# Two batches' kv products in one visit, twice, and a remainder tile drawn forward: attention and MLP in one Trainium2 kernel

## The chip, the cores and the metric

The kernel runs on one core of a Trainium2 chip. The metric is device microseconds (us) of one execution, as the median of several. The core has TensorE (PE in the profile, matrix products), VectorE (DVE), ScalarE (ACT), GpSimd (POOL), the sync engine (SP, which here only starts transfers) and 16 DMA engines, on which every transfer runs.

## The reference

For each of 8 batches and 8 heads of width 64, with 576 rows: an attention without a softmax, normalised by its root mean square, and then a block with a layer norm and two weights.

```python
kv  = einsum('bhsd,bhse->bhde', k, v)            # 64x64 per batch and head
o   = einsum('bhsd,bhde->bhse', q, kv)
x   = o / sqrt(mean(o*o, -1) + 1e-6) * g_norm    # then heads side by side: (8, 576, 512)
xn  = (x - mean(x)) / sqrt(var(x) + 1e-6) * g_ln
out = x + relu(xn @ w_ch1) @ w_ch2               # 512 -> 2048 -> 512
```

## The kernel before

**Tiles.** The 576 rows of a batch are four main tiles of 128 rows and a rest of 64. The rests of batches b-1 and b make one remainder tile, so there are four of them: 1, 3, 5 and 7, named by the higher batch (r1 to r7 below). The four remainder tiles are a ninth block of 512 rows, `"rem"`, that goes through the MLP last.

**Slots.** PE sets the pace. Its order is written out by hand: `mm1(b, 0, 4)` is 16 groups of four matmuls of 512 columns (a group fills one PSUM tile `p1`, of which there are three, and ACT evicts it with a relu at L419 into `m1`), and `mm2(b)` is four rows `ts` of 16 matmuls, each row in one of two PSUM tiles `p2`, which `finish` empties on DVE (L437) and stores through SP (L452, L453). Before each group of mm1 and each four matmuls of mm2 stands a `tick()`: this is a slot. From batch 3 on, batch b has mm1 in slots 32b to 32b+15 and mm2 in 32b+16 to 32b+31; `"rem"` has 256 to 287. Whatever else is to be done is entered with `at(slot, fn)`, and all its instructions are put on all engines' queues when that tick is reached. A slot thus fixes an order of instructions, not a time: POOL and SP, which have little to do, often reach an instruction long before PE reaches the slot it was entered at.

**What is entered at slots.**

- `load_batches` (POOL): first one or two 1x1 copies into `gate`, which wait for a transfer that has to come before, and then two DMAs for each tensor named. `k_in`, `v_in` and `q_in` have two buffers each, for even and odd batches.
- `turn_q_dma(b)`: DVE copies q of a batch into `q_p` in another order (L204), and SP starts one DMA transpose of it into `qt` (L206). `qt` has four buffers.
- `kv_of(*bs)`: 40 matmuls on PE for each batch into the one PSUM tile `kv_ps` (L247), and then two copies on ACT for each batch (L252, L253) into `kv_pack[b % 4]`.
- `plan_tile(s, make, turn_at, on_pe, x_at)` carries one tile through. At slot s: `o` (PE, L274, reads `qt` and `kv_pack`, writes one of two PSUM tiles `o_ps`), `sq` (ACT, L280), `red` (DVE, L301). At x_at, s+2 if it isn't given: `root` (ACT, L311), `inv`, `y` (DVE, L306, after which `o_ps` is free), `x`, `xc` (DVE, L325 to L335). At x_at+4: `var` (ACT, L343). At turn_at: a DMA transpose from SP into the block's `xT_blk` (L355), which mm1 reads.
- `rem_tile(b)` makes the remainder tile out of `qt` and `kv_pack` of batches b-1 and b.

mm1 of a batch can't start before the `xT_blk` of its four tiles has landed.

Of the kernel before, what the change touches and what calls it, by code (L numbers as in the profile page):

```python
# [14 lines left out]
def kernel(  # L15
# [18 lines left out]
    B, H, S, D = q.shape  # L34
# [57 lines left out]
    def load(dst, t, b, h0=0, h1=H):  # L92
        nc.gpsimd.dma_start(dst[:64, h0:h1], lo(t, b, h0, h1))
        nc.gpsimd.dma_start(dst[64:, h0:h1, :J], up(t, b, h0, h1))

    def load_batches(what, *after):
        for element in after:
            nc.gpsimd.tensor_copy(gate, element)  # L98
        tensors = {"k": (k_in, k), "v": (v_in, v), "q": (q_in, q)}
        for name, b in what:  # L100
            dst, src = tensors[name]
            load(dst[b % NB], src, b)
# [63 lines left out]
    qts, held, blks, rstds, m1s, q_ps = {}, {}, {}, {}, {}, {}  # L166
# [35 lines left out]
    def turn_q_dma(b):  # L202
        q_p = kv_in.tile([128, JJ, H, D], bf16, tag="qp", bufs=2)
        nc.vector.tensor_copy(q_p.rearrange("p j h d -> p h j d"), q_in[b % NB])  # L204
        q_t = qt_pool.tile([128, JJ, HP, 128], bf16, tag="qt", name="qt")
        nc.sync.dma_start_transpose(  # L206
            q_t.rearrange("p j hp t -> p (j hp) t"), q_p.rearrange("p j h d -> p (j h d)"))
        qts[b] = q_t
# [31 lines left out]
    def kv_of(*bs):  # L240
        kv_ps = ps_m.tile([128, len(bs), HP, D], f32, tag="misc", name="kv_ps")
        for i, b in enumerate(bs):
            for hp in range(HP):
                for j in range(JJ):
                    for hh in range(2):
                        h = 2 * hp + hh
                        nc.tensor.matmul(  # L247
                            kv_ps[hh * D:hh * D + D, i, hp, :], lhsT=k_in[b % NB][:, h, j, :],
                            rhs=v_in[b % NB][:, h, j, :], start=(j == 0), stop=(j == JJ - 1))
        for i, b in enumerate(bs):  # L250
            kvp = held[b] = kv_pack[b % 4]
            nc.scalar.copy(kvp[:D, :, :D], kv_ps[:D, i])  # L252
            nc.scalar.copy(kvp[D:, :, D:], kv_ps[D:, i])  # L253

    def new_block(n, bufs):
        x_blk = xpool.tile([128, 4, Dm], f32, tag=f"x{n}", bufs=bufs, name="x_blk")
        st_blk = xpool.tile([128, 3, 4], f32, tag=f"st{n}", bufs=bufs, name="st_blk")
        xT_blk = xpool.tile([128, nK, 512], bf16, tag=f"xT{n}", bufs=bufs, name="xT_blk")
        return x_blk, st_blk, xT_blk
# [98 lines left out]
    def main_tile(b, j, pool=None, tag="ops"):  # L358
        q_t, kvp = qts[b], held[b]
        if b not in blks:  # L360
            blks[b] = new_block("main", 3)
        return Tile([(slice(0, 128), lambda hp: q_t[:, j, hp, :], kvp)], blks[b], j, pool, tag)

    def rem_tile(b):
        mms = []
        for half, bb in enumerate((b - 1, b)):
            qt, kp = qts.pop(bb), held.pop(bb)
            mms.append((slice(half * 64, (half + 1) * 64),
                        lambda hp, qt=qt: qt[:, J, hp, :64], kp))
        if "rem" not in blks:  # L370
            blks["rem"] = new_block("rem", 1)
        return Tile(mms, blks["rem"], b // 2)

    def plan_tile(s, make, turn_at, on_pe, x_at=None):
        box = []

        def first():
            t = make()
            box.append(t)
            t.o()  # L380
            t.sq()
            t.red()

        def second():
            t = box[0]
            t.y()
            t.x()
            t.xc()

        def third():  # L390
            box[0].var()

        def fourth():
            box[0].turn(on_pe)

        at(s, first)
        at(x_at or s + 2, second)
        at((x_at or s + 2) + 4, third)
        at(turn_at, fourth)
# [22 lines left out]
    def rstd_of(b):  # L422
        rstd = work.tile([128, 4], f32, tag="rstd", bufs=3, name="rstd")
        nc.scalar.activation(rstd, blks[b][1][:, 2, :], func=AF.Sqrt, scale=1.0 / Dm, bias=eps_sb)  # L424
        nc.vector.reciprocal(rstd, rstd)  # L425
        rstds[b] = rstd
# [47 lines left out]
    def at(slot, fn):  # L474
        agenda.setdefault(int(slot), []).append((slot, fn))
# [162 lines left out]
    def turned_q(b):  # L638
        return qts[b][:1, J, HP - 1, 127:]

    at(47, lambda: load_batches((("k", 3), ("v", 3), ("q", 3)), turned_q(2)))
    at(68, lambda: load_batches((("k", 4), ("v", 4), ("q", 4)),
                                turned_q(3), blks[2][2][:1, nK - 1, 511:]))
    at(100, lambda: load_batches((("k", 5), ("v", 5), ("q", 5)), turned_q(4)))
    at(132, lambda: load_batches((("q", 6), ("k", 6), ("v", 6), ("k", 7), ("v", 7)),
                                 turned_q(5)))
    at(164, lambda: load_batches((("q", 7),), turned_q(6)))


    at(115, lambda: kv_of(5))  # L650
    for s, bs, rem, x_at, tn in ((56, (3,), 1, 64, 69), (85, (4,), 3, 88, 94),
                                 (152, (6, 7), 5, 154, 160)):
        at(s, lambda bs=bs: kv_of(*bs))
        plan_tile(s + .1, lambda rem=rem: rem_tile(rem), tn, False, x_at)
    plan_tile(210, lambda: rem_tile(7), 216, False)


    for b, at_q, at_o, step in ((3, 56.05, 67, 4.3), (4, 86, 97, 4.75),
                                *((b, 32 * b - 43.3, 32 * b - 32, 5) for b in range(5, B))):
        at(at_q, lambda b=b: turn_q_dma(b))  # L660
        for j in range(J):
            o = at_o + step * j
            plan_tile(o, lambda b=b, j=j: main_tile(b, j), o + 6, False)
        at(32 * b + 14, lambda b=b: rstd_of(b))
# [59 lines left out]
```

## Time and profile before

| | |
|---|---|
| median of 3 runs | 288.96 us (288.90 to 289.06) |
| the profiled execution's own time | 288.75 us |
| its span, first to last instruction | 286.7 us |
| around the span | 2.05 us |
| PE busy | 277.8 us, 97% of the span |
| DVE, ACT, POOL busy | 150.0, 152.9, 43.1 us |
| read from HBM, written | 36.71 MB, 9.44 MB |

Times in the views are microseconds from the start of the span. In the chain that ended last, every piece has its start, its length, and the engine with the tile written and the source line; "issue" is time in which nothing that the profile shows was waited for. In a timeline, the bracket at the end of a row says how long the engine had stood idle before it, and for whom. A DMA's row in a timeline is its issue; the time from there to landing is in the view of DMAs.

### The profile page before, as it was taken

Reading aid. Unit: us, or ns where it says so; the run is one execution under the profiler, and the core shown is the slowest. Engines: PE = TensorE matmul, PEld = TensorE weight load, DVE = VectorE, ACT = ScalarE, POOL = GpSimd, SP = SyncE. Lnnn points to the kernel's source line nnn. Section 1 sums busy time; section 2 is a strip of 40 time slices with the busy share of each in tenths; the row PEclk is TensorE's granted clock in tenths of the full one; section 3 lists DMA queues with packets and bytes.
Section 4 is the critical chain, followed back from the end, with each engine's and each line's share of the span. In section 5 each row is a group of like instructions: output and inputs, shape, how many; then the busy total and the mean of one; then the engine's idle time right before and its main releaser. Section 6 shows DMA issues by size and latency. Waiting matters only on the chain.

```text
span 286.7 us, 5727 instructions
## 1 busy us (share of the span) xinstructions
PE 277.8 (97%) x2269; PEld 158.0 (55%) x2295; DVE 150.0 (52%) x331; ACT 152.9 (53%) x333; POOL 43.1 (15%) x73
## 2 busy tenths in 40 slices
PE   7889999999999999999999999999999999999995
PEld 3579755995579654454444544444444444444444
DVE  5774119937997883774376475763679200220022
ACT  3477844995468643971387338911893066016500
POOL 8522510041036005000710020000000000000000
PEclk9999999999999999999999999999999999999999
DMA  7999999969997979986999995047203410230033
GB/s 215 198 209 202 201 191 197 214 111 188 144 180 124 185 141 172 214 101 127 159 215 190 120 160 135 18 82 158 56 18 72 95 37 0 48 81 19 0 73 76
DMA packets 67419, 36.76 MB, mean 128 GB/s; under 512 B 35517, under 2 KB 62525, under 8 KB 67393
## 3 DMA queue, kind: packets, MB, share of 16 engines
q0 software_dynamic: 28720, 18.29, 44.2%
q1 hardware_dynamic: 38160, 17.39, 30.4%
q10 hardware_dynamic: 512, 0.72, 0.8%
q8 instruction: 18, 0.29, 0.5%
q14 instruction: 9, 0.07, 0.1%
HBM read 36.71 MB, written 9.44 MB: 161 GB/s over the span
## 4 chain that ended last, share of the span: by engine, by line
PE 91%; DMA 2%; DVE 2%; ACT 2%; issue 1%; DVEq 0%; POOLq 0%
PE p L432 43%; PE p L416 42%; PE o_ps L274 3%; DMA v_in<-in_v_dram 2%; PE kv_ps L247 2%; ACT m L419 1%; DVE x_blk L292 0%; DVE xc L552 0%; ACT xT_blk L353 0%; PE tp L351 0%; ACT rms L311 0%; PE odd L226 0%; DVE ss L518 0%; PE tp L559 0%; DVE ss L301 0%
## 5 line engine op out<-in xcount | busy, mean ns | idle before, releaser
L416 PE MATMUL p<-xT_blk,w_sb 128*128 128x128 bf16 (+2 forms) x1015 | 131.2, 285 | 0.9
L432 PE MATMUL p<-w_sb,m 128*128 128x512 bf16 (+2 forms) x592 | 126.2, 368 | 1.2 <-issue 0.5
L419 ACT ACTIVATE m<-p 128x512 bf16<-128x512 f32 x144 | 85.2, 596 | 46.7 <-PE p L416 44.3
L416 PEld LDWEIGHTS <-w_sb 128*128 128x128 bf16 x1024 | 78.6, 98 | 44.5 <-issue 1.1
L432 PEld LDWEIGHTS <-m 128*128 128x128 bf16 x608 | 57.3, 98 | 62.9
L437 DVE SCALAR_TENSOR_TENSOR o_sb<-p,rstd,x_blk 128x512 f32<-128x512 f32 (+2 forms) x38 | 27.2, 721 | 47.7 <-PE p L432 42.1
L280 ACT ACTIVATE sq<-o_ps 128x512 f32<-128x512 f32 x35 | 20.9, 596 | 26.7 <-PE o_ps L274 26.5
L343 ACT ACTIVATE dev<-x_blk,st_blk 128x512 f32<-128x512 f32 x36 | 25.7, 714 | 13.1 <-DVE st_blk L329 13.1
L301 DVE TENSOR_REDUCE ss<-sq 128x8 f32<-128x512 f32 x35 | 23.7, 678 | 17.0 <-ACT sq L280 17.0
L335 DVE SCALAR_TENSOR_TENSOR xc<-x_blk,st_blk,g_ln_sb 128x512 bf16<-128x512 f32 x34 | 25.6, 752 | 1.2
L306 DVE TENSOR_TENSOR y<-o_ps,inv 128x512 f32<-128x512 f32 x33 | 22.8, 692 | 3.1
L325 DVE SCALAR_TENSOR_TENSOR x_blk<-y,g_norm_sb 128x512 f32<-128x512 f32 x33 | 22.8, 692 | 1.1
L318 DVE RECIPROCAL inv<-rms 128x8 f32<-128x8 f32 x36 | 7.3, 202 | 23.3 <-ACT rms L311 23.3
L425 DVE RECIPROCAL rstd<-rstd 128x4 f32<-128x4 f32 x9 | 1.6, 175 | 29.9 <-ACT rstd L424 29.8
L311 ACT ACTIVATE rms<-ss,eps_sb 128x8 f32<-128x8 f32 x36 | 10.6, 295 | 11.5 <-DVE ss L301 11.3
L274 PEld LDWEIGHTS <-qt 128*128 128x128 bf16 (+1 forms) x156 | 10.3, 100 | 6.0 <-issue 0.4
L274 PE MATMUL o_ps<-kv_pack,qt 128*128 128x128 bf16 (+1 forms) x156 | 13.6, 220 | 0.0
L98 POOL COPY gate<-qt 1x1 bf16<-1x1 bf16 x5 | 0.9, 177 | 82.4 <-DMA qt<-q_p 82.4
L199 PE MATMUL p<-fill_sb 128*128 128x512 bf16 x26 | 7.8, 452 | 1.3 <-DVE eps_sb L138 1.2
L252 ACT CAST kv_pack<-kv_ps 64x256 bf16<-64x256 f32 x7 | 2.6, 366 | 10.7 <-PE kv_ps L247 10.7
L343 ACT ACTIVATION_READ_ACCUMULATOR dev<-x_blk,st_blk 128x1 f32 x36 | 6.8, 190 | 0.0
L247 PEld LDWEIGHTS <-k_in 128*64 128x64 bf16 x280 | 4.9, 112 | 2.4 <-issue 2.3
(82 smaller groups left out, 112.6 us busy)
## 6 DMA issues: line engine op xcount, KB each, us to landing
out_dram<-o_sb SPq DMA_DIRECT2D x66, 128.0 KB, 2.6
w_sb<-in_moe_w_ch_dram POOLq DMA_DIRECT2D x8, 512.0 KB, 15.2
q_in<-in_q_dram POOLq DMA_DIRECT2D x7, 320.0 KB, 9.7
k_in<-in_k_dram POOLq DMA_DIRECT2D x7, 320.0 KB, 8.7
v_in<-in_v_dram POOLq DMA_DIRECT2D x7, 320.0 KB, 10.3
q_in<-in_q_dram POOLq DMA_DIRECT2D x8, 256.0 KB, 10.5
k_in<-in_k_dram POOLq DMA_DIRECT2D x7, 256.0 KB, 9.3
v_in<-in_v_dram POOLq DMA_DIRECT2D x7, 256.0 KB, 12.3
```

The lines of the kernel that those rows point to most:

```text
L247: nc.tensor.matmul(kv_ps[hh * D:hh * D + D, i, hp, :], lhsT=k_in[b % NB][:, h, j, :], rhs=v_in[b % NB][:, h, j, :], start=(j == 0), stop=( ...
L274: nc.tensor.matmul(flat[rows, hp * 128:(hp + 1) * 128], lhsT=lhsT_of(hp), rhs=kvp[:, hp, :], start=True, stop=True)
L280: nc.scalar.activation(self.sq_t, self.o_ps, func=AF.Square)
L301: nc.vector.tensor_reduce(self.ss, self.sq_t, axis=AX.X, op=ALU.add)
L306: nc.vector.tensor_mul(self.y_t, self.o_ps, self.inv().to_broadcast([128, H, D]))
L325: nc.vector.scalar_tensor_tensor(x_blk[:, ts].rearrange("p (h d) -> p h d", h=H), in0=self.y_t, scalar=1.0, in1=g_norm_sb.to_broadcast([12 ...
L335: nc.vector.scalar_tensor_tensor(self.xc_t, in0=x_blk[:, self.ts], scalar=st[:, 1, self.ts:self.ts + 1], in1=g_ln_sb, op0=ALU.add, op1=ALU ...
L343: nc.scalar.activation(dev, x_blk[:, ts], func=AF.Square, bias=st[:, 1, ts:ts + 1], accum_out=st[:, 2, ts:ts + 1])
L416: nc.tensor.matmul(p1[:, i, :], lhsT=w1_sb[:, kk, de * 128:(de + 1) * 128], rhs=blk[2][:, kk, sl], start=(kk == 0), stop=(kk == nK - 1))
L419: nc.scalar.activation(m1[:, de0:de0 + per, sl], p1, func=AF.Relu)
L432: nc.tensor.matmul(p2[:, c0:c1], lhsT=m1s[b][:, de, ts * 128:(ts + 1) * 128], rhs=w2_sb[:, de, c0:c1], start=(de == 0), stop=(de == nDe - 1))
L437: nc.vector.scalar_tensor_tensor(o_sb[:, c0:c1], in0=p2[:, c0:c1], scalar=rstds[b][:, ts:ts + 1], in1=blks[b][0][:, ts, c0:c1], op0=ALU.mu ...
```

## The change

Batch 5's kv product is no longer made by itself at slot 115: it is made with batch 4's, at slot 93 instead of 85, and r3 moves with it. The products of 6 and 7 move from slot 152, in mm2 of batch 4, to slot 161, in mm1 of batch 5, with 7 made ahead of 6; r5 moves with them, and r7 follows it there instead of standing at slot 210. k and v of batch 5 are loaded behind q of 4, k and v of 6 behind q of 5, and q of 7 together with q of 6. The q turns of batches 4, 6 and 7 move from slots 86, 148.7 and 180.7 to 92, 147 and 151, and the main tiles of batch 4 from 97 and steps of 4.75 to 101 and steps of 4.3, those of 6 from 160 and steps of 5 to 165 and steps of 4.5. `rem_tile` keeps the q and kv of its two batches until later where they are those of r7. The number of instructions on PE is the same; POOL has one gate copy less.

```diff
@@ rem_tile @@
-            qt, kp = qts.pop(bb), held.pop(bb)
+            qt, kp = qts[bb], held[bb]
+            if b < B - 1:
+                del qts[bb], held[bb]
@@ kernel body @@
-    at(68, lambda: load_batches((("k", 4), ("v", 4), ("q", 4)),
+    at(68, lambda: load_batches((("k", 4), ("v", 4), ("q", 4), ("k", 5), ("v", 5)),
                                 turned_q(3), blks[2][2][:1, nK - 1, 511:]))
-    at(100, lambda: load_batches((("k", 5), ("v", 5), ("q", 5)), turned_q(4)))
-    at(132, lambda: load_batches((("q", 6), ("k", 6), ("v", 6), ("k", 7), ("v", 7)),
+    at(101, lambda: load_batches((("q", 5), ("k", 6), ("v", 6)), turned_q(4)))
+    at(132, lambda: load_batches((("q", 6), ("q", 7), ("k", 7), ("v", 7)),
                                  turned_q(5)))
-    at(164, lambda: load_batches((("q", 7),), turned_q(6)))

-    at(115, lambda: kv_of(5))
-    for s, bs, rem, x_at, tn in ((56, (3,), 1, 64, 69), (85, (4,), 3, 88, 94),
-                                 (152, (6, 7), 5, 154, 160)):
+    for s, bs, rem, x_at, tn in ((56, (3,), 1, 64, 69), (93, (4, 5), 3, 95, 101),
+                                 (161, (7, 6), 5, 162, 168)):
         at(s, lambda bs=bs: kv_of(*bs))
         plan_tile(s + .1, lambda rem=rem: rem_tile(rem), tn, False, x_at)
-    plan_tile(210, lambda: rem_tile(7), 216, False)
+    plan_tile(161.2, lambda: rem_tile(7), 170, False, 164)

-    for b, at_q, at_o, step in ((3, 56.05, 67, 4.3), (4, 86, 97, 4.75),
-                                *((b, 32 * b - 43.3, 32 * b - 32, 5) for b in range(5, B))):
+    for b, at_q, at_o, step in ((3, 56.05, 67, 4.3), (4, 92, 101, 4.3),
+                                (5, 116.7, 128, 5), (6, 147, 165, 4.5), (7, 151, 192, 5)):
         at(at_q, lambda b=b: turn_q_dma(b))
```

## The prediction

> **What bounds the kernel now.** I read the page's busy times first, then the chain that ended last, then the timelines of ACT, DVE and POOL around the pieces that move. TensorE is the bound, and nearly all of the chain is its own:
>
> ```profile
> PE 277.8 (97%) x2269; PEld 158.0 (55%) x2295; DVE 150.0 (52%) x331; ACT 152.9 (53%) x333; POOL 43.1 (15%) x73
> ...
> PE 91%; DMA 2%; DVE 2%; ACT 2%; issue 1%; DVEq 0%; POOLq 0%
> ```
>
> From 33 us on PE hardly stops. So work taken off ACT, DVE or DMA gains nothing; only PE work taken away gains, and every wait that reaches PE is paid in full. A 512-column matmul costs 0.2158 us: mm2(5), which has nothing entered in it, starts at 185.11 in the chain and ends at 198.92, 13.81 us for 64. A slot is four, 0.863 us. The pieces that the change moves stand in the chain thus:
>
> ```profile
> 100.21 0.75 PE kv_ps L247 x40
> 100.96 0.23 PE o_ps L274 x8
> 101.19 0.16 issue
> ...
> 128.08 0.75 PE kv_ps L247 x40
> 128.84 0.16 issue
> ...
> 161.78 1.39 PE kv_ps L247 x80
> 163.16 0.23 PE o_ps L274 x8
> 163.39 0.32 PE p L432
> ...
> 215.36 0.34 PE o_ps L274 x8
> ```
>
> Here kv of 4 with r3, kv of 5, kv of 6 and 7 with r5, and r7. None waits for anything: 80 matmuls for two batches cost 1.39 us, 40 cost 0.75 and a gap of 0.16 behind them.
>
> What lies behind a kv product is in ACT's timeline, four copies that start 0.05 us after the last matmul and end at 164.72:
>
> ```profile
> 163.21 0.37 ACT L252 CAST kv_pack<-kv_ps 64x256 bf16<-64x256 f32 x1 [3.95 <-PE kv_ps L247]
> 163.58 0.37 ACT L253 CAST kv_pack<-kv_ps 64x256 bf16<-64x256 f32 x1
> 163.97 0.37 ACT L252 CAST kv_pack<-kv_ps 64x256 bf16<-64x256 f32 x1
> 164.35 0.37 ACT L253 CAST kv_pack<-kv_ps 64x256 bf16<-64x256 f32 x1
> ```
>
> The first two aren't earlier than the other batch's matmuls. Nobody waits for them now: r5 reads kv of 4 and 5, and batch 6 is read at 170.40.
>
> The load of k, v and q of batch 4 is issued from 88.22 (POOL's timeline), and its last half is issued at 91.61 and lands 10.6 us later, at 102.2 (the view of DMAs for that moment). A load of five tensors, from 137.61, has its last half issued at 145.65 and landing 14.0 us later, at 159.65:
>
> ```profile
> 91.61 0.75 POOL L94 DMA_DIRECT2D q_in<-in_q_dram  x1
> ...
> q_in<-in_q_dram POOLq DMA_DIRECT2D x1, 256.0 KB, 10.6
> ...
> 145.65 0.68 POOL L94 DMA_DIRECT2D v_in<-in_v_dram  x1 [1.12 <-DMA q_in<-in_q_dram]
> ...
> v_in<-in_v_dram POOLq DMA_DIRECT2D x1, 256.0 KB, 14.0
> ```
>
> **What the Trainium skill says.** (1) "TensorE: Matmul & The Clock Gate", Part 2, step-by-step: only weight loads are pulled ahead, matmuls stay in program order. So a matmul that waits holds up everything behind it. The trace agrees with that page's 215.7 ns between 512-column matmuls (215.8 here). (2) "PSUM — Partial Sum Buffer", Engine vs sequencer instructions: ScalarE and VectorE are strict FIFO. The trace agrees: mm2(2)'s first row ends on PE near 99.4, and its finish starts on DVE at 100.97, straight behind tile (3,3)'s xc. (3) "DMA: Bandwidth & Descriptors", Issuing engines are not separate DMA queues: POOL's loads and SP's stores and transposes share the 16 engines. The trace agrees: 188 GB/s from 92 to 94 us with loads nearly alone, 184 from 94 to 96 with over a quarter of the bytes a transpose's.
>
> **The change part by part.**
>
> *Fewer visits: a gain of 0.6.* PE has the same instructions, so only the gaps go. By the chain the pieces cost now 1.13 (100.21 to 101.34), 0.92, 1.61 and 0.34, together 4.00. After: kv of 4 and 5 with r3 like the present pair, 1.61; the pair with r5, and r7 at 0.23, 1.84. That saves 0.55. By whole mm2 stretches against the empty one of 13.81 (14.90, 14.68, 15.53, 14.48 now) the pieces cost 4.35, and 1.72 and 1.95 after: 0.68. I take 0.6, ends 0.4 and 0.7.
>
> *kv of 5 at slot 93 waits for its load: +1.3.* Slot 80 starts at 95.89 and nothing is entered between it and slot 93 but a q copy on DVE, so slot 93 starts at 95.89 + 13 x 0.863 = 107.1, and the first matmul of batch 5 is due 0.7 later, at 107.8. k and v of 5 are queued straight behind q of 4 (POOL issues them from about 92.3 to 95; the buffers are long free). q of 4 lands at 102.2. In the load of five tensors the last two landed at 156.5 and 159.65, 6.4 us after the third (153.25), with transposes running beside them. 102.2 + 6.4 = 108.6. Beside them now run two stores of 0.26 MB, part of a third, and tile (3,3)'s transpose: a little over half a MB at some 190 GB/s would be 3 us if all were taken from the load, but the 6.4 already holds a share of such traffic. I take 109.1: PE waits 1.3. Ends: 0.3 (the DMA engines were idle in part from 102 to 107) and 2.6 (the same five-tensor load from its first issue, 22.0 us, gives 110.25). Behind it on PE is r3, mm2(2)'s last row and everything else.
>
> *Main tiles of 4 in steps of 4.3: +0.8.* The last `o` goes from slot 111.25 to 113, one slot into mm2(3), and the tiles follow each other in 4.3 slots, 3.93 us with the `o`. DVE needs 3.3 us for a tile, and about 1 us of idling for the `root` on ACT, which is in a queue with relus: 4.2, so it falls behind. The present steps of 4.3 (batch 3) show by how much (the chain, then DVE's timeline):
>
> ```profile
> 94.79 0.22 PE o_ps L274 x4
> ...
> 100.30 0.75 DVE L335 SCALAR_TENSOR_TENSOR xc<-x_blk,st_blk,g_ln_sb 128x512 bf16<-128x512 f32 x1
> 100.97 0.75 DVE L437 SCALAR_TENSOR_TENSOR o_sb<-p,rstd,x_blk 128x512 f32<-128x512 f32 x1
> ```
>
> From the end of `o` at 95.01 to the finish behind that tile's xc, 5.96 us; with steps of 4.75 (batch 4 now, `o` ends 124.63, finish 129.84) it was 5.21. In the new order the finish of mm2(3)'s first row stands behind xc of tile (4,3). It ends 5.96 + 0.75 = 6.7 us after `o`, and a little more (6.9 by laying out the rows in turn, as r3 is in this queue too). PE needs its p2 for the third row at slot 120, 7 slots or 6.04 us after `o`: a wait of 0.7 to 0.9. I take 0.8; ends 0.2 and 1.1.
>
> *r7 behind kv of 7 and 6: +1.4.* r7's first matmul reads kv_pack of 6, which ACT copies last. With the kv matmuls ending at 0, the copies end at 164.72 - 163.16 = 1.56 and PE sees it at 1.6; r5's `o` covers 0.23. PE waits 1.4. ACT has slot 160's relu (0.6) ahead of the copies, hidden by the 1.39 of kv. Ends 1.2 and 1.6: the order of rows leaves nothing else to run.
>
> *ACT and DVE in mm1(5): +1.0.* Now the visit is in mm2(4), where ACT has no relus. At slot 161 it has one per slot of 0.863 us (0.49 from start to start), and r5, r7 and tile (6,0) all come within four slots, each 1.5 us of ACT (sq 0.60, rms 0.20, var 0.70) and 3.3 us of DVE. From 0 as above, by the durations in the timelines: sq of r5 ends 2.2, red 2.9; sq of r7 2.8, red 3.6; DVE has r5's inv to xc from 3.8 to 6.4, r7's to 9.0, and only then red of (6,0), to 9.7. But ACT comes to rms of (6,0) at 8.3 and stands there until 9.75 with relus queued behind. PE has three p1: its group 170 could start at 10.1 and waits for relu 167 (to 10.6), group 171 for relu 168 behind var of r7, 172 for 169: 0.5 + 0.3 + 0.2 = 1.0. I take 1.0; ends 0 (rows a little shorter) and 1.7.
>
> *Costed at nothing.* q of 7 turned at 151: SP issues two q transposes of 3.2 us, with a pair of stores and tile (5,3)'s transpose between them. That one is issued about 4.5 us after q of 6 and lands 3.0 later, as now; by my layout about 1 us before slot 160 needs it. If that cover is gone PE waits up to 1 there. Loads of q 5, k 6, v 6 (gate at about 113) and q 6, q 7, k 7, v 7 (gate near 142, landed by 160) are needed from 131, 159 and 172. Stores queued behind q of 7 wait 3 us, and o_sb has four buffers. r7's old place at 210 and the last stretch have nothing that waits. r3's x at 95 is in DVE's queue ahead of batch 4.
>
> Sum: -0.6 + 1.3 + 0.8 + 1.4 + 1.0 = **+3.9**. Against the profiled execution, 286.7 + 2.05 = 288.75, that is 292.65; the median stands 0.2 higher, so 292.9.
>
> **The rivals.**
>
> *Only r7's wait is paid.* k and v of 5 arrive in time and the queues absorb the rest: +1.4 - 0.6 = +0.8, 289.8, and with one of the small waits up to 290.5. For it: 5 us with little DMA work from 102 to 107. Against: two tensors need 6.3 us at 188 GB/s alone.
>
> *The merge pays: faster.* PE saves the 0.6 to 0.7 of gaps: 288.3. It decides if the waits put in stay under 0.6 in all, at slot 161 above all: the copies there would have to be over about 0.8 us after the kv matmuls. For it: the copies of 7 are first, and could run under the matmuls of 6, and would take 0.7 out of the wait. Against: the pair now in the trace shows all four copies after the last matmul. Short of that it ends as no change.
>
> *A longer wait.* Loads and stores collide at slot 93 for over 3 us, or both q transposes delay (5,3). A fourth place, the TensorE page's Part 1, says that PE's clock falls to half after an idle window of about 3.4 us; no run here shows it (the granted clock is 1.00 everywhere). That would cost an estimated 1.7 more: +6 to +8, 295 to 297.
>
> **How the numbers follow.** No change is taken as within 0.2%, 0.6 us, about what a measurement of this kernel can tell. The forecast (two or more of the new waits) has 0.70, and its own terms at their ends, not all at once, give +1.8 to +6.5; r7's wait alone 0.16, of which 0.03 lies within 0.2%; the merge that pays 0.06, 0.04 faster and 0.02 within; the longer wait 0.08. So faster 0.04, within 0.2% 0.05, slower 0.91. For 8 in 10 the range goes from 289.9, which takes in most of the second case, to 295.6.
>
> **What would show it.** In the chain after: idle of PE at kv_ps near 107.8 for DMA v_in or k_in; at o_ps near 171 to 173 for ACT kv_pack, 1.4 us; p waiting for DVE o_sb near slot 120 and for ACT m in mm1(5). PE busy stays within 1 us of 277.8. It is wrong if L247 never waits, if r7 doesn't, or if PE stands for long anywhere else, at slot 160 above all.

## The result: slower by 3.4%, most of it in one wait

| | before | after |
|---|---|---|
| median of 4 runs | 288.93 us (288.52 to 289.06) | 298.77 us (297.74 to 299.51) |
| ratio, 95% interval | | 1.0341 (1.0306 to 1.0375) |
| the profiled execution, its span | 288.75, 286.7 us | 299.51, 297.4 us |
| PE busy | 277.8 us | 280.7 us |

Executions of the changed kernel differ by some us, since the wait at slot 93 and TensorE's clock behind it differ from one to the next. A number from one execution is therefore called that here, and a median stands beside it where the verdict needs it. A run over 1.5% above the shortest of its own kernel counts as slow and is left out of a ratio; two runs below are, both of "r7 out of slot 161" at 210.

The page after, the same two lines as before and the row of the clock (tenths of full speed, in 40 slices of 7.4 us):

```profile
PE 280.7 (94%) x2269; PEld 159.3 (54%) x2295; DVE 149.5 (50%) x331; ACT 152.4 (51%) x333; POOL 42.9 (14%) x72
...
PEclk9999999999999995999999999999999999999999
...
PE 77%; DMA 10%; DVE 6%; ACT 3%; issue 2%; POOL 0%; DVEq 0%; POOLq 0%
```

PE has the same 2269 matmuls, yet is busy 2.9 us longer, and its clock stands at a half in one slice. DMA has 10% of the chain instead of 2%. PE's waits, in us in total, times and longest (waits before 33 us, which both kernels have, left out):

```profile
PE kv_ps L247 <- DMA v_in<-in_v_dram: 5.5, 1, 5.5
PE o_ps L274 <- ACT kv_pack L253: 1.4, 1, 1.4
...
PE p L434 <- DVE o_sb L439: 0.7, 1, 0.7
...
PE p L418 <- ACT m L421: 0.5, 2, 0.3
```

These are the four places that the prediction named, and no fifth of that length. Their pieces in PE's timeline (`o`, mm1 and mm2 are now L274, L418 and L434):

```profile
107.21 0.82 PE L247 MATMUL kv_ps<-v_in,k_in 128*64 128x64 bf16 x40
113.50 1.28 PE L247 MATMUL kv_ps<-v_in,k_in 128*64 128x64 bf16 x40 [5.46 <-DMA v_in<-in_v_dram]
...
141.54 7.07 PE L434 MATMUL p<-w_sb,m 128*128 128x512 bf16 x31 [0.66 <-DVE o_sb L439]
...
180.97 0.41 PE L274 MATMUL o_ps<-kv_pack,qt 128*64 128x128 bf16 x8 [1.37 <-ACT kv_pack L253]
...
190.00 1.02 PE L418 MATMUL p<-xT_blk,w_sb 128*128 128x512 bf16 x4 [0.30 <-ACT m L421]
191.19 2.86 PE L418 MATMUL p<-xT_blk,w_sb 128*128 128x512 bf16 x11 [0.16 <-ACT m L421]
```

The second row shows both halves of the miss. Batch 5's matmuls stand 5.46 us for v. Then they take 1.28 us where batch 4's 40, the same work, took 0.82. By the stretches around it (PE and PEld busy, DVE, ACT, POOL, then PEclk, DMA share and GB/s), the granted clock is half from 111 to 118:

```profile
core 0: us, PE busy (x) PEld busy (x) DVE busy (x) ACT busy (x) POOL busy (x), PEclk, DMA share, GB/s
107.00:111.00 4.00, 1.03 (x41) 0.71 (x40) 0.94 (x2) 0.00 (x0) 0.00 (x0) 1.00 1.41 169
111.00:114.00 3.00, 0.50 (x19) 0.53 (x21) 0.00 (x0) 0.00 (x0) 0.00 (x0) 0.52 1.23 263
114.00:118.00 4.00, 3.67 (x43) 2.00 (x41) 0.69 (x1) 2.37 (x6) 1.57 (x4) 0.51 0.43 92
118.00:122.00 4.00, 4.00 (x20) 1.85 (x19) 3.16 (x7) 1.30 (x3) 2.68 (x4) 1.00 1.21 153
```

Length of each stage, from the first matmul of one to the first of the next:

| us | mm2(2) | mm1(3) | mm2(3) | mm2(4) | mm1(5) | mm2(5) | mm2(6) | all ten |
|---|---|---|---|---|---|---|---|---|
| before | 14.68 | 14.71 | 14.89 | 15.75 | 14.48 | 14.04 | 14.26 | |
| after | 22.99 | 14.48 | 15.08 | 13.81 | 18.88 | 14.26 | 13.81 | |
| more | +8.31 | -0.23 | +0.19 | -1.94 | +4.40 | +0.22 | -0.45 | +10.50 |

The others, mm1(2), mm1(4) and mm1(6), are the same. So the first half of the change (batches 4 and 5, r3) costs +8.3 and the second (6 and 7, r5, r7) +2.2.

### The profile page after: what moved, and what is told of

Same layout as the page of the kernel before. It is cut to its first block, busy times and chain, and to the rows that moved or that the text cites. A ratio compares the mean times of both kernels' runs of the same rounds, so it can differ in the third digit from the quotient of the medians.

```text
span 297.4 us, 5723 instructions
## 1 busy us (share of the span) xinstructions
PE 280.7 (94%) x2269; PEld 159.3 (54%) x2295; DVE 149.5 (50%) x331; ACT 152.4 (51%) x333; POOL 42.9 (14%) x72
## 4 chain that ended last, share of the span: by engine, by line
PE 77%; DMA 10%; DVE 6%; ACT 3%; issue 2%; POOL 0%; DVEq 0%; POOLq 0%
PE p L434 36%; PE p L418 35%; DMA v_in<-in_v_dram 8%; PE o_ps L274 2%; DMA k_in<-in_k_dram 2%; PE kv_ps L247 2%; ACT m L421 1%; DVE x_blk L325 1%; DVE y L306 1%; DVE xc L335 1%; DVE ss L301 1%; ACT rms L311 1%; ACT dev L343 1%; DVE x_blk L292 0%; DVE xc L554 0%
## 5 line engine op out<-in xcount | busy, mean ns | idle before, releaser
L418 PE MATMUL p<-xT_blk,w_sb 128*128 128x128 bf16 (+2 forms) x1015 | 131.8, 285 | 1.5 <-ACT m L421 0.5
L434 PE MATMUL p<-w_sb,m 128*128 128x512 bf16 (+2 forms) x592 | 127.7, 370 | 1.9 <-DVE o_sb L439 0.7
L418 PEld LDWEIGHTS <-w_sb 128*128 128x128 bf16 x1024 | 78.5, 98 | 45.8 <-issue 2.4
L434 PEld LDWEIGHTS <-m 128*128 128x128 bf16 x608 | 57.9, 98 | 64.8 <-issue 3.0
L274 PE MATMUL o_ps<-kv_pack,qt 128*128 128x128 bf16 (+1 forms) x156 | 13.8, 224 | 1.4 <-ACT kv_pack L253 1.4
L274 PEld LDWEIGHTS <-qt 128*128 128x128 bf16 (+1 forms) x156 | 10.6, 103 | 7.0 <-DMA qt<-q_p 1.5
L247 PE MATMUL kv_ps<-v_in,k_in 128*64 128x64 bf16 x280 | 6.0, 203 | 5.6 <-DMA v_in<-in_v_dram 5.5
L252 ACT CAST kv_pack<-kv_ps 64x256 bf16<-64x256 f32 x7 | 2.6, 366 | 16.6 <-PE kv_ps L247 16.5
## 6 DMA issues: line engine op xcount, KB each, us to landing
q_in<-in_q_dram POOLq DMA_DIRECT2D x7, 320.0 KB, 10.1
v_in<-in_v_dram POOLq DMA_DIRECT2D x7, 320.0 KB, 13.7
```

The lines of the kernel that those rows point to most:

```text
L247: nc.tensor.matmul(kv_ps[hh * D:hh * D + D, i, hp, :], lhsT=k_in[b % NB][:, h, j, :], rhs=v_in[b % NB][:, h, j, :], start=(j == 0), stop=( ...
L274: nc.tensor.matmul(flat[rows, hp * 128:(hp + 1) * 128], lhsT=lhsT_of(hp), rhs=kvp[:, hp, :], start=True, stop=True)
L418: nc.tensor.matmul(p1[:, i, :], lhsT=w1_sb[:, kk, de * 128:(de + 1) * 128], rhs=blk[2][:, kk, sl], start=(kk == 0), stop=(kk == nK - 1))
L434: nc.tensor.matmul(p2[:, c0:c1], lhsT=m1s[b][:, de, ts * 128:(ts + 1) * 128], rhs=w2_sb[:, de, c0:c1], start=(de == 0), stop=(de == nDe - 1))
```

## The experiments

All start from the changed kernel unless another is named. "+7.1" behind a median is its distance from the median of the kernel before, measured beside it on the same chip.

**The whole again.** No edit: a reference on the chip on which the halves ran.

> The changed kernel once more, so that the two halves below stand beside it on one chip. 298.8 us, 297.5 to 299.5 as before. Theory (the wait for v of 5 at slot 93 differs from execution to execution, and the clock falls only behind a long one): the executions spread by over 1 us, and the longer ones have the lower mean clock.

Measured: 299.34 (298.07 to 299.95), +10.4, ratio 1.0357 (1.0327 to 1.0387); v is waited for 5.32 us.

**The halves.** First only the half of batches 4 and 5, then only that of 6 and 7.

```diff
@@ first half alone @@
-    at(132, lambda: load_batches((("q", 6), ("q", 7), ("k", 7), ("v", 7)),
+    at(132, lambda: load_batches((("q", 6), ("k", 7), ("v", 7)),
+    at(164, lambda: load_batches((("q", 7),), turned_q(6)))
-    (161, (7, 6), 5, 162, 168)
+    (152, (6, 7), 5, 154, 160)
-    plan_tile(161.2, lambda: rem_tile(7), 170, False, 164)
+    plan_tile(210, lambda: rem_tile(7), 216, False)
-    (6, 147, 165, 4.5), (7, 151, 192, 5)
+    (6, 148.7, 160, 5), (7, 180.7, 192, 5)
@@ second half alone @@
-    at(68, lambda: load_batches((("k", 4), ("v", 4), ("q", 4), ("k", 5), ("v", 5)),
+    at(68, lambda: load_batches((("k", 4), ("v", 4), ("q", 4)),
-    at(101, lambda: load_batches((("q", 5), ("k", 6), ("v", 6)), turned_q(4)))
-    at(132, lambda: load_batches((("q", 6), ("q", 7), ("k", 7), ("v", 7)),
+    at(100, lambda: load_batches((("k", 5), ("v", 5), ("q", 5)), turned_q(4)))
+    at(132, lambda: load_batches((("q", 6), ("q", 7), ("k", 6), ("v", 6), ("k", 7), ("v", 7)),
+    at(115, lambda: kv_of(5))
-    (93, (4, 5), 3, 95, 101)
+    (85, (4,), 3, 88, 94)
-    (4, 92, 101, 4.3)
+    (4, 86, 97, 4.75)
```

> The kernel before with the first half of the change alone: kv of 4 and 5 with r3 at slot 93, k and v of 5 loaded behind q of 4, k and v of 6 behind q of 5, tiles of 4 at 101 in steps of 4.3; batches 6 and 7 and r7 as before. By the stages of the two profiles, mm2(2) gains 8.3 (less where the wait is shorter), mm1(3) and mm2(3) nothing: 296 to 297 us. Rival (the halves aren't additive, the second is paid by the first): under 294 or over 298.5.

Measured: 296.08 (295.45 to 296.37), +7.1.

> The kernel before with the second half of the change alone: kv of 7 and 6 with r5 and r7 at slot 161, q of 7 loaded with q of 6 and turned at 151, tiles of 6 at 165 in steps of 4.5; batches 4 and 5 as before. By the stages of the two profiles, mm2(4) loses 1.9, mm1(5) gains 4.4, mm2(5) gains 0.2 and mm2(6) loses 0.45: +2.2, so 290.9 us, with 1.4 us of idle at o_ps for kv_pack. Rival (it also hides behind the delay of the first half, as the six tensors loaded at once and the two q turns need the time that the delay gives): over 292 us, with idle for DMA.

Measured: 292.65 (291.19 to 293.17), +3.7. The sum, 10.8, is near the whole's 10.4: two thirds of the loss lie in the first half. The second half alone missed its 290.9, and what came is the rival's case: over 292, with PE idle for a DMA. PE's timeline there:

```profile
172.44 0.22 PE L274 MATMUL o_ps<-kv_pack,qt 128*64 128x128 bf16 x1 [1.37 <-ACT kv_pack L253]
173.37 0.63 PE L274 MATMUL o_ps<-kv_pack,qt 128*64 128x128 bf16 x7 [0.71 <-DMA qt<-q_p]
```

Here r7 waits for q of 7's transpose too, 0.71 us, which it doesn't in the whole change; the load at 132 has six tensors here instead of four, though that this is the reason was not tried. And the clock falls to half for one piece of 3.41 us, at 173.18, behind two waits of 2.08 us together. Three of its four runs have a mean clock of 0.993 or 0.994, what one such piece comes to; the fourth, at 1.0, took 291.19, close to the expectation.

**Only kv of 5 taken out of slot 93.**

```diff
-    (93, (4, 5), 3, 95, 101)
+    (93, (4,), 3, 95, 101)
+    at(115, lambda: kv_of(5))
```

> The changed kernel with kv of 5 by itself at slot 115, as before the change; its load stays queued behind q of 4. Theory (PE waits 5.5 us at slot 93 for v of 5, and its clock is halved for the 6.8 us behind that, worth about 2.0): both go, one kv visit more costs 0.25, so about 298.8 - 7.3 = 291.5 us, clock 1.00 all through, no idle of kv_ps for DMA. Rival (the longer load in that stretch disturbs the stores and transposes whoever waits for it): most of the time stays, over 295 us.

Measured: 292.74 (292.60 to 292.90), +4.1, clock 1.0 in every run, no wait at `kv_ps`. This one move is 5.7 to 6.3 of the 9.8 to 10.4 us. The 1.2 us above the expectation are partly a wait that the long one had covered, and partly that the expectation took the 7.3 us of the longest of the four executions from the median (298.8 instead of 299.5). Waits of the profiled execution:

```profile
PE o_ps L274 <- ACT kv_pack L253: 1.4, 1, 1.4
...
PE p L434 <- DVE o_sb L439: 0.9, 1, 0.9
PE p L418 <- DMA xT_blk<-xc: 0.5, 1, 0.5
PE p L418 <- ACT m L421: 0.5, 2, 0.3
```

mm1(3) now waits 0.5 for the transpose of tile (3,3), which runs beside the same load.

**The pair four slots later.** `(93, (4, 5), 3, 95, 101)` becomes `(97, (4, 5), 3, 99, 105)`.

> The changed kernel with kv of 4 and 5 and r3 at slot 97 instead of 93 (r3's steps four slots later too). The visit comes 3.45 us later, so the wait for v of 5 should shrink from 5.5 to about 2.0 us. Theory (the halved clock follows from the long idle): the clock stays at 1.00 and its 2.0 us go as well: 298.8 - 3.4 - 2.0 = 293.4 us. Rival (the clock drop has another cause, or the load lands the later for it): 295.4 us or more, with the clock still halved for some us.

Measured: 293.81 (293.65 to 294.50), +5.2, clock at least 0.999. As expected in size, but the wait left over is not v's: v is there, and slot 96 waits 1.5 us for tile (3,3)'s transpose. PE's wait in this kernel:

```profile
PE p L418 <- DMA xT_blk<-xc: 1.5, 1, 1.5
```

The piece of its chain ahead of slot 96 (start, length, the transfer from issue to landing):

```profile
103.15 8.21 DMA xT_blk<-xc
```

It takes 8.21 us; in the kernel before, the same transpose is issued at 103.62, with no load beside it, and takes 2.5. So moving the pair to slot 97 doesn't win it all back: the early load's second victim stands at slot 96.

**The wait kept, the clock kept up.** 25 matmuls on constant data, their results thrown away, between the products of 4 and 5.

```diff
@@ kv_of, loop over i @@
+            if bs == (4, 5) and i == 1:
+                fill(25)
```

> The changed kernel with 25 matmuls of 512 columns on zeros between kv of 4 and kv of 5, 5.4 us of PE work whose result is thrown away, put into the wait of 5.5 us. Theory (the clock is halved because PE stood idle): the wait is as long but filled, the clock stays at 1.00, and the time falls by the 2.0 us of slow matmuls, to 296.8 us. Rival (the clock drop is not tied to that idle time, or costs nothing): 298.8 us or more.

PE's timeline:

```profile
107.78 5.57 PE L199 MATMUL p<-fill_sb 128*128 128x512 bf16 x24
113.28 0.82 PE L249 MATMUL kv_ps<-v_in,k_in 128*64 128x64 bf16 x40
```

Batch 5's matmuls start at 113.28, as late as in the changed kernel (113.50), but take 0.82 instead of 1.28, and mm2(2) takes 20.93 instead of 22.99: the clock alone was 2.06 us in that execution, as expected. The median, 298.09 (297.63 to 298.27), +9.4, missed the 296.8 expected and is only 0.7 below the changed kernel's. The expectation took 2.0 us from the median, while the 2.06 are from the longest of the changed kernel's four executions; in the others the wait may have been shorter than the filling, which would fit, but their waits are not on record.

**What the load waits for.** v of 5's last half is issued at 95.38 and lands 18.0 us later. Beside it run SP's transfers (SP's timeline; L454 and L455 are the stores of batch 2's rows, L355 tile (3,3), L206 q of 4):

```profile
101.92 0.47 SPq L454 DMA_DIRECT2D out_dram<-o_sb  x1
102.43 0.59 SPq L455 DMA_DIRECT2D out_dram<-o_sb  x1
103.07 1.29 SPq L355 DMA_TRANSPOSE xT_blk<-xc  x1
104.46 0.54 SPq L454 DMA_DIRECT2D out_dram<-o_sb  x1
105.04 0.60 SPq L455 DMA_DIRECT2D out_dram<-o_sb  x1
107.24 0.47 SPq L454 DMA_DIRECT2D out_dram<-o_sb  x1
107.75 1.14 SPq L455 DMA_DIRECT2D out_dram<-o_sb  x1
109.00 4.87 SPq L206 DMA_TRANSPOSE qt<-q_p  x1
```

Three kernels leave these out, in part: the stores of the first three rows of batch 2; the transposes of two tiles of batch 3 (a fill with zeros on DVE stands for each); both.

```diff
@@ finish: no stores @@
+        if b == 2 and ts < 3:
+            return
@@ plan_tile, tiles (3,2) and (3,3): no transposes @@
-            box[0].turn(on_pe)
+            nc.vector.memset(box[0].blk[2][:, :, ...], 0.0)
```

> The changed kernel without the stores of the first three row tiles of batch 2 (that part of the output is left out), 0.79 MB of which 0.6 to 0.7 pass between 102 and 113 us, while k and v of 5 are under way. Theory (v of 5 lands late since the stores take the engines from it): v of 5 lands 2.5 us earlier, PE waits about 3, 295 to 296 us. Rival (what slows it are the transposes, or the load by itself): the wait stays over 4.5 us, 298 us or more.

> The changed kernel without the DMA transposes of tiles (3,2) and (3,3), the last two of batch 3 (their part of xT_blk is set to zero on DVE, so that part of the output is not the reference's). They pass beside k and v of 5 from about 98 to 110 us. Theory (stores and transposes together make v of 5 late, 2.5 us by the stores, the rest by the transposes): v of 5 lands 1.5 to 2.5 us earlier, near 111, PE waits 3 to 4: 296 to 297.5 us. Rival (the rest of the delay is the load's own): it lands as late as before, near 113, 298 us or more.

> Both left out: the stores of the first three row tiles of batch 2, and the transposes of tiles (3,2) and (3,3). Theory: with the engines to itself the load lands where the forecast had it, v of 5 near 109, PE waits about 1.3 us, the clock stays, and 0.7 of wait at slot 120 and 1.4 of r7's and 0.5 in mm1(5) remain: 298.8 - 4.2 - 2.1 = 292.5 us. Rival (the load of five tensors is slow by itself or starts too late): PE waits over 2.5 us, 294.5 us or more.

Batch 5's row in PE's timeline without the stores:

```profile
110.55 0.82 PE L247 MATMUL kv_ps<-v_in,k_in 128*64 128x64 bf16 x40 [2.79 <-DMA v_in<-in_v_dram]
```

The same without the transposes:

```profile
110.90 1.28 PE L247 MATMUL kv_ps<-v_in,k_in 128*64 128x64 bf16 x40 [2.87 <-DMA v_in<-in_v_dram]
```

And without either:

```profile
109.48 0.82 PE L247 MATMUL kv_ps<-v_in,k_in 128*64 128x64 bf16 x40 [1.76 <-DMA v_in<-in_v_dram]
```

Medians 295.85 (294.50 to 297.40), 296.65 (294.26 to 297.26) and 293.47 (293.14 to 294.69): +7.1, +7.8 and +4.6. Against some +10.1 for the whole, the mean of its two measurements, that is 3.0, 2.3 and 5.5 less, clock included. The shares add up, and no run of the first two is as long as the shortest of the changed kernel (297.74). With both gone the load lands at about 109.3, close to the 109.1 that the prediction took for the load with the traffic beside it. One landing alone would not show the share of either: in eight profiled executions with all of this traffic (the changed kernel twice, the first half, the filled wait, r7 at 210, kv of 5 taken out, r7 at 163, the pair at 97) v lands between 110.4 and 113.4, without the stores at 110.4, without the transposes at 110.8. Only the landing with neither, 109.3, lies outside; for each by itself it is the medians that speak.

**The load issued earlier.** Its second gate, the tile of batch 2 that must have been turned first, is left out of `load_batches` at 68.

> The changed kernel without the second gate copy (for the transpose of tile (2,3)) ahead of the load of batch 4 and k, v of 5, so that POOL issues it from about 85.6 instead of 88.4 us. Theory (the load is a queue of bytes that is worked off at the rate of the DMA engines, and starts too late): v of 5 lands 2.5 us earlier, PE waits 2.5 to 3 instead of 5.4, at most 3.4 us of halved clock: 294.5 to 296 us. Rival (before 90 us the engines are taken by transposes, so an earlier issue only shares with them): it lands under 1 us earlier, 298 us or more, or mm1 waits for xT_blk instead.

Measured: 295.90 (294.28 to 298.61), +7.2. The median is where the theory had it, but one run of the four is as long as the changed kernel's, and that is the profiled one. POOL's timeline shows why in it an issue 2.7 us earlier doesn't bring landing forward by as much:

```profile
85.64 0.71 POOL L93 DMA_DIRECT2D k_in<-in_k_dram  x1 [0.52 <-issue]
...
92.19 0.68 POOL L93 DMA_DIRECT2D v_in<-in_v_dram  x1 [1.05 <-DMA k_in<-in_k_dram]
95.18 0.68 POOL L94 DMA_DIRECT2D v_in<-in_v_dram  x1 [2.31 <-DMA k_in<-in_k_dram]
```

The first DMA starts at 85.64 instead of 88.38, but v's last two wait on POOL for an earlier k to land, and the last is issued at 95.18, 0.2 earlier than in the changed kernel; it lands at about 112.0 and PE waits 4.16. The records of the semaphores (the counters that tell a landing) say which k: the load's ten DMAs use eight semaphores in turn, so the ninth and the tenth carry those of the first two, the halves of k of 4, and v's last half is issued 0.3 us after the second of these has landed (94.90; in the changed kernel 95.09, issue at 95.38).

**q of 4's turn later.** `(4, 92, 101, 4.3)` becomes `(4, 95, 101, 4.3)`.

> The changed kernel with the q turn of batch 4 at slot 95 instead of 92, so that DVE's copy and SP's transpose stand behind r3 and so behind the wait. Theory (stores and the transposes of x before it slow the load; q's transpose is issued at 109 and has moved little before v lands): the wait falls by 0.5 us or less, 298 to 299 us. Rival (the transpose is what holds the load up near 108.5, where the engines stand almost still): the wait falls by over 2 us, under 296 us.

Measured: 302.39 (301.12 to 303.81), +13.7. Both theories were off. Waits of PE:

```profile
PE kv_ps L247 <- DMA v_in<-in_v_dram: 4.3, 1, 4.3
PE o_ps L274 <- DMA qt<-q_p: 2.4, 1, 2.4
```

v lands at 111.9 and its wait is 1.2 less than in the changed kernel, within what both vary without this edit, and the turn, now issued only at 120.08, makes the first tile of batch 4 wait 2.4. It says little on the turn's share of the load.

**r7 out of slot 161.** First back at 210, then at 163.2 (from the kernel with kv of 5 alone).

```diff
-    plan_tile(161.2, lambda: rem_tile(7), 170, False, 164)
+    plan_tile(210, lambda: rem_tile(7), 216, False)
@@ the other, with kv_of(5) at 115 @@
+    plan_tile(163.2, lambda: rem_tile(7), 172, False, 165)
```

> The changed kernel with r7 back at slot 210. Theory (r7 waits 1.4 us on PE for the last kv_pack copy, and its work crowds ACT in mm1(5) for 0.5): 298.8 - 1.4 - 0.5 + 0.1 = 297.0 us, no idle of o_ps for kv_pack. Rival (the queues behind slot 161 were not slowed by r7; its own q, landing near 180, or the kv visit in mm1 holds PE): under 0.5 us less, 298.3 or more.

Measured: 292.38 and 295.31 at a mean clock of 0.999 and 0.993, and 297.43 and 297.80 at 0.988, as low as the changed kernel goes with two pieces at half clock (0.989). The median of the four is 296.37, +7.7; the ratio of the first two is 1.0179 (1.0120 to 1.0238). With such a spread the total says little on r7, and the stage has to: nothing waits in mm1(5), which takes 16.20 instead of 18.88, both at full clock. r7 there costs 2.7 us, of which 1.4 and 0.5 are its two waits and 0.23 its own matmuls. The profiled execution is the shortest, 292.38: v lands at 110.44 in it, PE waits 2.28, and the clock stays at full speed.

> a1_kv5_alone with r7 two slots later, at 163 (its second step at 165, its turn at 172). Theory (1.4 us of its time is PE standing before r7 until the kv_pack copies are over): 292.7 - 1.4 = 291.3 us, no idle of o_ps. Rival (mm1(5) is bound by ACT and DVE there, so the wait comes back as waits of p for ACT): 292.3 us or more, with over 1.5 us of idle of p for ACT m.

Measured: 293.54 (293.08 to 294.36), +4.6 where kv of 5 alone had +4.1, and not the 291.3 that the theory gave: the rival's case. r7 no longer waits for `kv_pack`, and PE waits for relus instead (its timeline):

```profile
180.93 1.02 PE L418 MATMUL p<-xT_blk,w_sb 128*128 128x512 bf16 x4 [0.64 <-ACT m L421]
...
184.12 1.89 PE L418 MATMUL p<-xT_blk,w_sb 128*128 128x512 bf16 x8 [1.19 <-ACT m L421]
186.29 1.89 PE L418 MATMUL p<-xT_blk,w_sb 128*128 128x512 bf16 x8 [0.28 <-ACT m L421]
```

2.1 us, where the changed kernel has 1.4 + 0.5 = 1.9. As this reads, the wait for the copies had given ACT time for its relus.

**r7 well apart.** The second half alone, with r7 at 184.2 and its turn at 193.

```diff
-    plan_tile(161.2, lambda: rem_tile(7), 170, False, 164)
+    plan_tile(184.2, lambda: rem_tile(7), 193, False)
```

> b2_second_half with r7 at slot 184, in mm2(5), where ACT has no relus. Theory (what the second half loses is all r7: its wait for kv_pack and q of 7, the clock behind that, and its load on ACT and DVE in mm1(5)): mm2(4) -1.94, mm1(5) +1.72, mm2(5) +0.45, mm2(6) -0.45 against before, so 288.7 us, from 288.4 to 289.2, as good as the kernel before. Rival (a kv visit in mm1 costs by itself, as its copies push the relus back): 290 us or more, with idle of p for ACT m.

Measured over 12 runs: 289.31 (288.60 to 289.78) against 288.74, ratio 1.0012 (1.0001 to 1.0023): 0.57 us above the kernel before by the medians and 0.1 above the range expected, and the same as before within the 0.2% that can be told apart. In its timeline the pair and r5 go through without a bracket, but mm1(5) starts with one:

```profile
169.24 1.04 PE L418 MATMUL p<-xT_blk,w_sb 128*128 128x512 bf16 x4 [0.38 <-DMA xT_blk<-xc]
170.20 1.46 PE L247 MATMUL kv_ps<-v_in,k_in 128*64 128x64 bf16 x80
171.49 0.39 PE L274 MATMUL o_ps<-kv_pack,qt 128*64 128x128 bf16 x8
171.82 2.55 PE L418 MATMUL p<-xT_blk,w_sb 128*128 128x512 bf16 x10
```

The 0.38 is slot 160's wait for a tile's transpose, which the prediction had named and set at nothing. The move of 6, 7 and r5 to slot 161 thus costs some 0.6 us at most; drawing r7 to it costs the other 3, clock included. No version ran faster than the kernel before.

**The runs together.** mm2(2) has 13.81 of its own and 1.72 for the pair with r3 (a pair with r5 adds as much to mm1(5) where nothing waits: 16.20 - 14.48). With the wait taken off as well, what remains is the clock's price. Each row is the profiled execution; "busy" is PE's share of one window of 3.41 us, explained below:

| | v of 5 lands | PE waits | busy | at half clock | mm2(2) | mm2(2) - 15.53 - wait |
|---|---|---|---|---|---|---|
| changed kernel | 113.4 | 5.46 | 0.10 | 6.83 | 22.99 | 2.0 |
| the same again | 113.4 | 5.32 | 0.00 | 6.83 | 23.21 | 2.4 |
| q of 4's turn later | 111.9 | 4.29 | 0.18 | 6.83 | 22.26 | 2.4 |
| load earlier | 112.0 | 4.16 | 0.18 | 6.83 | 22.19 | 2.5 |
| first half alone | 112.0 | 4.04 | 0.06 | 3.41 | 21.10 | 1.5 |
| no transposes | 110.8 | 2.87 | 0.31 | 3.41 | 19.64 | 1.2 |
| no stores | 110.4 | 2.79 | 0.40 | 0 | 18.30 | 0.0 |
| r7 at 210 | 110.4 | 2.28 | 0.45 | 0 | 17.78 | 0.0 |
| neither stores nor transposes | 109.3 | 1.76 | 0.72 | 0 | 17.27 | 0.0 |

The stage is explained to 0.1 us wherever the clock stays up. The last column is 0, 1.2 to 1.5, or 2.0 to 2.5 with none, one or two pieces at half clock; less than half of their length, since PE still waits in a part of it.

The length of the wait alone doesn't decide on the fall: 2.79 us had none, 2.87 one piece, 4.04 one and 4.16 two. The clock's records say more. In each trace the record of the clock begins at full speed a few us after the start (at 5.29 in the changed kernel), and every change comes a whole number of windows of 3.413 us after that: each fall in the table after 31 windows (105.8 us), the fall of the second half alone after 49. The start of this grid differs from one execution to the next (from 4.6 to 6.5 us in the table's nine), so the same wait can lie in one window or be cut in two. "busy" is the window just before the 31 are over. It fell where PE was busy for 0.31 of it or less, and not at 0.40 or more. The second piece came where PE was busy for 0.50 or less of the first, and not at 0.76 or more. Stretches of that window, in the changed kernel and in the second half alone (by its own grid):

```profile
107.69:111.10 3.41, 0.34 (x22) 0.23 (x16) 0.25 (x1) 0.00 (x0) 0.00 (x0) 1.00 1.42 154
...
169.77:173.18 3.41, 1.52 (x77) 1.19 (x71) 0.14 (x1) 2.39 (x6) 0.00 (x0) 1.00 0.84 169
```

The second is 0.44 busy, most of it with short matmuls, and the clock fell. So there is no one share of busy time at which it falls in all cases.

## Why the prediction was right in sign and wrong in size

It forecast 292.9, with 289.9 to 295.6 for 8 cases in 10; it is 298.77. Slower was right, and each of the four waits came where it was said to. Step by step:

- **"kv of 5 at slot 93 waits for its load: +1.3" is the step that failed.** Slot 93 came when it should (40 matmuls of batch 4 from 107.21), and the load was issued as read (to 95.4). It landed at 113.4 and not at 109.1: a wait of 5.46 in the profiled execution, 2.3 to 5.5 over the profiled ones with the same work before them, ends forecast 0.3 and 2.6. The wrong term is the competition: the prediction took 6.4 us for the last two tensors from a load "with transposes running beside them" and added only 0.5 for the stores and the transpose here. These 6.9 us, from the landing of q of 4 to that of v of 5, were 10.1 (103.22 to 113.36). With stores and tile transposes away they were 7.3 (102.07 to 109.34), and by the medians the two cost 3.0 and 2.3 us, clock included. That they share the engines the prediction had itself cited ("DMA: Bandwidth & Descriptors", Issuing engines are not separate DMA queues); the runs without them show it, and what was wrong was to price it from one load in another stretch. "The DMA engines were idle in part from 102 to 107" was read from the kernel before, where the load that the change puts there doesn't run.
- **The clock, not in the sum: 2.1 in the profiled execution.** It stood only in the rival "a longer wait", at 0.08, with an estimate of 1.7 from the Trainium skill, "TensorE: Matmul & The Clock Gate", Part 1. The filled wait shows the mechanism and its price: 22.99 - 20.93 = 2.06. A wait at slot 93 that leaves PE idle for most of one window of the clock then costs more than itself. With 5.46 instead of 1.3, and 2.1, this step has 6.2 of the 6.9 us missed (299.51 - 292.65). That rival ended at 295 to 297, so it was right in kind and still short: it reckoned with one piece at half clock, and there were two.
- **"Fewer visits: a gain of 0.6" is not to be seen.** With r7 back at 210, mm2(2) to mm2(3) less their waits last 44.40 (17.78 + 14.48 + 15.08 - 2.28 - 0.66) against 44.28 before (14.68 + 14.71 + 14.89). A gain of some 0.2 could hide there, as a bracket can be that much shorter than what its wait costs (with neither stores nor transposes 1.76, and 1.96 from start to start). mm2(4) to mm2(6) without mm1(6), where that kernel merges no visit, last 58.54 (13.81 + 16.20 + 14.26 + 14.27) against 58.53. The reading was at fault: of the 64 matmuls of mm2(2) and of mm2(3) the chain before has only 62 each (19 + 43, and 12 + 49 + 1), and one without a record fits into each 0.16 of "issue" that was read as a gap. Without these two the pieces sum to 3.68 before and 3.45 after, a gain of 0.2. And mm2(6) before is 14.26 from first matmul to first matmul, not 14.48. That the 0.6 did not come is most of the rest of the miss.
- **"Main tiles of 4 in steps of 4.3: +0.8"**: 0.66 and, with kv of 5 elsewhere, 0.9. Right.
- **"r7 behind kv of 7 and 6: +1.4"**: 1.37, to the copy. Right as a wait; but taking it away by itself brought nothing, which the sum didn't say (r7 at 163). It and the next step are one cost: r7 in that stretch.
- **"ACT and DVE in mm1(5): +1.0"**: waits of 0.3 and 0.16, about half. The two steps together were 2.4; mm1(5) without r7 is 2.7 shorter, r7's own matmuls among it.
- **"Costed at nothing"**: in the changed kernel q of 7's turn and tile (5,3) indeed let slot 160 go through. In the second half alone, with a longer load at 132, r7 waited 0.71 for q of 7, so that cover is thin; and with r7 well apart slot 160 waited 0.38 for its tile. The transpose of tile (3,3), not looked at as something that PE could wait for, takes 8.2 us beside the load instead of 2.5 and lands up to 1.5 us late for slot 96; in the changed kernel the 5.46 hides it.

Open is why v lands when it does to the last us. POOL issues its last half only behind the landing of the second half of k of 4, at 93.9 to 96.2 over four executions with the same work before it, and it lands 16.6 to 18.0 us after that. The DMA engines also stand nearly idle for 0.5 to 1 us near 108.5 in the changed kernel with the load not done. This was seen, and not explained.

## What to carry to other kernels

When a load is moved forward into a stretch where stores and DMA transposes run, add their transfers to its landing time in full before calling it covered; a gap in the old profile's DMA row is no proof of room. A single wait of some 3 us or more on PE should be priced with the clock loss behind it, here 1.2 to 2.5 us depending on how it lay to the clock's windows. A short gap of "issue" in the chain may be a matmul without a record: count the records before a gain is built on it. A tile drawn into a stretch where ACT and DVE are full is paid for there even if its own wait is taken away.

## What the runs showed of the hardware

- Behind these waits the granted clock fell to a half for 3.41 us or twice that, 6.83, and nothing between, and only at whole numbers of 3.413 us after its record begins (31 and 49). This agrees with the window that the TensorE page's Part 1 states (about 3.4 us). The page speaks of an idle window; here one piece followed two waits of 1.37 and 0.71 us that had a matmul between them, 2.08 us in all, and none followed waits of 2.28 and 2.79. The measured rows decide: the fall can come where PE was busy for 0.31 or 0.44 of a window.
- Matmuls on constant data in the wait, 5.57 us of them, left the clock at 1.0 (0.998 in one execution).
- Beside the load of k and v of 5, a DMA transpose of 128 rows took 8.2 us from issue to landing, where the same one took 2.5 in the kernel before, and the load's last half between 15.0 and 18.0 us, depending on what ran beside it.
